# Two of the first four x blocks transposed by DMA instead of the PE, V moved between Q and K of the first quarter, and the range check's matmul moved among the last projections

## The chip, the cores and the metric

The kernel runs on one core of one Trainium2 chip. The metric is the device time of one execution in microseconds (us), as the median of several; lower is better. The executions of one kernel in one set agree within about 0.4%, with a mean granted TensorE clock of 0.997 to 1.000. PE is TensorE, ACT is ScalarE, DVE is VectorE, POOL is GpSimd and SP is SyncE.

## The reference

Two independent problems, A and B, are computed and their results concatenated. Each is sliding-window attention with 2048 tokens, model width 1024, 32 heads of 32, window 256, in bfloat16:

```python
qkv = (x @ wqkv).reshape(B, S, 3, H, Dh).transpose(2, 0, 3, 1, 4)   # S 2048, H 32, Dh 32
scores = einsum("bhqd,bhkd->bhqk", q, k) * Dh ** -0.5
mask = (i - j >= 0) & (i - j < 256)
p = softmax(where(mask, scores, -1e9))
o = einsum("bhqk,bhkd->bhqd", p, v)
return o.transpose(0, 2, 1, 3).reshape(B, S, D) @ wo               # for A and B, then concatenated
```

## The kernel before

The work is a list of 180 *slots*. A slot makes the scores of four (key block, query block) pairs on the PE into one PSUM tile `st` of four banks, and ACT takes the exponential of all of them in one instruction of 1.88 us. The rest of the slot's PE time is filled with P.V products of earlier slots and with *chains*: eight matmuls (or two times eight of half width) of a projection of Q, K, V or of the output. A greedy list in Python decides at build time how much of which chain goes into which slot.

Chains write into two alternating PSUM banks `pp`. When a chain ends, its bank is emptied ("evicted") by ACT or DVE, as a small clock model in the builder chooses:

```python
class _Clock:
    def chain(self):
        self.pe = max(self.pe, self.banks.pop(0))
    def evacuate(self, engines):
        best = min(engines, key=lambda e: max(getattr(self, e), self.pe) + COST[e])
        end = max(getattr(self, best), self.pe + 150.0) + COST[best]
        ...
def evacuate(out, in_, engines=("act", "dve")):          # L188
    if clock.evacuate(engines) == "act":
        nc.scalar.copy(out=out, in_=in_)                 # L190
    else:
        nc.vector.tensor_copy(out=out, in_=in_)
```

Projections need x transposed. The first quarter of x (512 tokens) arrives as rows, in four blocks, and the PE turns each block with eight 128x128 transposes (`flip`); ACT and DVE copy the halves back. Later quarters are transposed by DMA. The start, with filler matmuls (`keep_warm`) while the PE has no data:

```python
for a in range(QB):                                      # QB = 4
    nc.sync.dma_start(out=xrow[a], in_=problems[0][0][a * P:(a + 1) * P, :])
    if a == 1:
        load_wqk(0, 1, nc.sync)
load_wv(0, 0, CT, nc.sync)
new_x(0, 1); load_x(0, 1)                                # next quarter, by DMA transpose
...
keep_warm(6)
flip(0); keep_warm(4); flip(1); keep_warm(3)
first(0, 0)                     # Q of columns 0..255
flip(2); flip(3)
first(1, 0); first(0, 256); first(1, 256)                # K, Q, K
emit(0, chains[0].size)                                  # V of blocks 0, 1
```

A range check guards the softmax without a maximum: bits of all Q and K are or-ed, and at the end one 1x1 matmul sums a flag over the partitions and DVE compares it:

```python
def decide(pool):
    csum = pool.tile([P, 512], F32, name="pp")
    nc.tensor.matmul(csum[0:1, 0:1], lhsT=ones1[:], rhs=okp[:], start=True, stop=True)
    nc.vector.tensor_scalar(out=unsafe_i[:], in0=csum[0:1, 0:1], ...)
```

After the last scores come a few P.V products and some 48 us of output projections alone, each chain of eight taking 1.73 us. I call that the *tail*.

## Time and profile before

| | before |
|---|---|
| median of 3 runs (range) | 609.61 us (609.18 to 610.35) |
| span of the profiled execution | 607.6 us |
| first projection of the second x quarter | 15.92 us |
| start of the last scores | 553.75 us |
| start of the last ACT cast | 602.25 us |

The last three rows cut the span at points that both programs have in common: before the first, all work of quarter 0 and the first scores are done in either program; after the second there remains the tail. So I compare *start* (up to 15.92), *body* (553.75 - 15.92 = 537.83) and *tail* (602.25 - 553.75 = 48.50) one by one.

The busy table, the start's chain of waits, the PE's waits and the check's lines are in the prediction below. Two more views of the kernel before are needed. First, the PE's timeline at the end of the start. The columns are start, length, engine, line, operation, output and inputs, shape, and count; in brackets would stand the idle time before it.

```profile
11.99 1.91 PE L172 MATMUL pp<-wv,xT 128*128 128x256 bf16 x16
13.83 0.40 PE L451 MATMUL st<-qT,kT 32*128 32x384 bf16 x8
14.16 1.92 PE L172 MATMUL pp<-wv,xT 128*128 128x256 bf16 x16
15.92 0.81 PE L172 MATMUL pp<-xT,wqk 128*128 128x512 bf16 x2
```

Nothing stands in brackets: V, the first scores, V again and the second quarter follow one another. The last line is my mark for the end of the start. Secondly, the SP queue's own timeline (the time that the issuing took):

```profile
3.77 8.07 SPq L133 DMA_TRANSPOSE xT<-in_A_x_dram  x1
13.12 6.00 SPq L133 DMA_TRANSPOSE xT<-in_A_x_dram  x1
```

Each of these DMAs transposes 1 MB and held its queue for 6 to 8 us here. The first of them brings the second quarter of x; it landed 10.2 us after its issue, at 14.0, and was wanted at 15.92.

### The profile page before, as it was taken

The page shows a single profiled execution, that of the slowest core. Times are in us where ns is not written, and L with a number is a line of the kernel's source. Part 1 is how long each engine was busy: PE and PEld are TensorE (multiplying, and loading weights), DVE is VectorE, ACT ScalarE, POOL GpSimd, SP SyncE. Part 2 cuts the span into 40 slices and gives each one's busy share as a digit, 9 for nine tenths or more (in the row PEclk, how much of TensorE's full clock was granted, in tenths as well). Part 3 has the DMA queues.
Part 4 walks back from the last instruction along what each step waited for, and adds up shares of the span by engine and source line. Part 5 has one row for each costly group of instructions (what it writes and reads, how often), then busy time and mean ns, then how long its engine had stood idle before and what let it go on. Part 6 is the DMA issues. An engine that isn't in the chain of part 4 may idle for free.

```text
span 607.6 us, 28768 instructions
## 1 busy us (share of the span) xinstructions
PE 593.6 (98%) x12786; PEld 344.3 (57%) x12838; DVE 468.4 (77%) x1199; ACT 441.1 (73%) x376; POOL 326.3 (54%) x630
## 2 busy tenths in 40 slices
PE   8999999999999999999999999999999999999996
PEld 6555466656655756564556756655455665545443
DVE  1677889898898898897888887898888887897200
ACT  3778887788888887877778877777776777785332
POOL 0565666665666666556555565555555655554000
PEclk9999999999999999999999999999999999999999
DMA  9833110111015501442111100112021040113222
GB/s 234 182 92 89 37 38 3 38 38 39 3 38 90 114 14 30 82 101 77 38 37 38 38 4 8 33 37 81 2 68 34 4 106 21 55 58 120 72 79 64
DMA packets 86802, 35.47 MB, mean 58 GB/s; under 512 B 65552, under 2 KB 86160, under 8 KB 86672
## 3 DMA queue, kind: packets, MB, share of 16 engines
q1 hardware_dynamic: 85632, 33.31, 22.2%
q8 instruction: 102, 1.67, 1.2%
q10 hardware_dynamic: 1040, 0.26, 0.2%
q14 instruction: 28, 0.23, 0.1%
HBM read 17.83 MB, written 8.39 MB: 43 GB/s over the span
## 4 chain that ended last, share of the span: by engine, by line
PE 96%; ACT 2%; issue 1%; DMA 1%; ACTq 0%
PE pp L176 44%; PE pp L172 28%; PE acc L513 13%; PE st L451 10%; ACT pt L459 1%; DMA oT<-in_A_x_dram 1%; PE acc L582 0%; PE pp L568 0%; ACT kT L190 0%; ACT vt L190 0%; PE st L582 0%; ACT osb L190 0%; PE pp L805 0%; ACTq L190 0%
## 5 line engine op out<-in xcount | busy, mean ns | idle before, releaser
L459 ACT ACTIVATE pt<-st 128x2048 bf16<-128x2048 f32 x180 | 338.0, 1878 | 91.6 <-PE st L451 73.5
L471 POOL TENSOR_SCALAR_AFFINE_SELECT pt<-pt 128x512 bf16<-128x512 bf16 x224 | 154.5, 690 | 145.7 <-ACT pt L459 143.1
L467 POOL TENSOR_SCALAR_AFFINE_SELECT pt<-pt 128x512 bf16<-128x512 bf16 x256 | 179.2, 701 | 85.8 <-ACT pt L459 85.8
L524 DVE RECIPROCAL rinv<-acc 128x128 f32<-128x128 f32 x128 | 122.0, 953 | 57.0 <-PE acc L513 56.4
L176 PE MATMUL pp<-xT,wqk 128*32 128x512 bf16 x2712 | 163.1, 379 | 0.0
L481 DVE TENSOR_TENSOR both<-pt 128x512 bf16<-128x512 bf16 x224 | 137.1, 651 | 0.0
L176 PEld LDWEIGHTS <-wqk 128*32 128x32 bf16 x2712 | 69.3, 97 | 54.2 <-issue 0.4
L172 PE MATMUL pp<-xT,wqk 128*128 128x512 bf16 (+1 forms) x323 | 76.7, 369 | 4.1 <-issue 2.4
L176 PE MATMUL pp<-wv,xT 128*32 128x256 bf16 x2436 | 75.9, 273 | 0.0
L451 PE MATMUL st<-qT,kT 32*128 32x384 bf16 (+2 forms) x1488 | 71.5, 269 | 0.1
L176 PEld LDWEIGHTS <-xT 128*32 128x32 bf16 x2436 | 63.8, 97 | 6.2
L529 DVE STREAM_SHUFFLE wide<-rinv 128x128 f32<-128x128 f32 x256 | 64.6, 298 | 0.0
L513 PE MATMUL acc<-pt,vt 128*32 128x128 bf16 (+1 forms) x2160 | 63.3, 239 | 0.0
L172 PE MATMUL pp<-wo_sb,oT 128*128 128x512 bf16 (+1 forms) x269 | 59.3, 373 | 1.3 <-issue 0.9
L451 PEld LDWEIGHTS <-kT 32*128 32x128 bf16 x1488 | 22.2, 92 | 64.5 <-issue 63.3
L190 ACT CAST osb<-pp 128x512 bf16<-128x512 f32 (+1 forms) x52 | 30.0, 577 | 39.1 <-PE pp L172 24.4
L531 DVE TENSOR_TENSOR oT<-acc,wide 128x256 bf16<-128x256 f32 x128 | 54.3, 425 | 4.4
L176 PE MATMUL pp<-wo_sb,oT 128*32 128x512 bf16 x952 | 55.6, 379 | 0.0
L172 PEld LDWEIGHTS <-wqk 128*128 128x128 bf16 x362 | 33.4, 98 | 37.0 <-issue 6.8
L172 PE MATMUL pp<-wv,xT 128*128 128x256 bf16 x415 | 50.9, 273 | 1.4 <-ACT kT L190 0.6
L513 PEld LDWEIGHTS <-vt 128*32 128x32 bf16 x2160 | 35.9, 96 | 26.4 <-issue 24.1
L172 PEld LDWEIGHTS <-xT 128*128 128x128 bf16 x415 | 38.9, 98 | 12.0 <-issue 6.1
(46 smaller groups left out, 386.5 us busy)
## 6 DMA issues: line engine op xcount, KB each, us to landing
out_dram<-osb SPq DMA_DIRECT2D x63, 128.0 KB, 1.8
wqk<-in_B_wqkv_dram SPq DMA_DIRECT2D x32, 128.0 KB, 2.5
wqk<-in_A_wqkv_dram SPq DMA_DIRECT2D x24, 128.0 KB, 2.7
wo_sb<-in_A_wo_dram SPq DMA_DIRECT2D x16, 128.0 KB, 2.2
wv<-in_B_wqkv_dram SPq DMA_DIRECT2D x16, 128.0 KB, 2.8
wo_sb<-in_B_wo_dram SPq DMA_DIRECT2D x16, 128.0 KB, 2.4
oT<-in_A_x_dram SPq DMA_DIRECT2D x4, 256.0 KB, 5.4
wv<-in_A_wqkv_dram SPq DMA_DIRECT2D x2, 512.0 KB, 5.9
```

The lines of the kernel that those rows point to most:

```text
L172: nc.tensor.matmul(out[:, lo:hi], lhsT=lhsT, rhs=rhs, start=start, stop=stop, skip_group_check=True)
L176: nc.tensor.matmul(out[c:c + 32, lo:hi], lhsT=lhsT[:, c:c + 32], rhs=rhs, start=start, stop=stop, tile_position=(0, c), skip_group_check=True)
L190: nc.scalar.copy(out=out, in_=in_)
L451: nc.tensor.matmul(st[:, r, a:b, :], lhsT=kT[32 * r:32 * r + 32, j * P:(j + 1) * P], rhs=qT[32 * r:32 * r + 32, q * P:(q + b - a) * P], st ...
L459: nc.scalar.activation(out=pt[:, :, :n, :].rearrange("p r a q -> p r (a q)"), in_=st[:, :, :n, :].rearrange("p r a q -> p r (a q)"), func= ...
L467: nc.gpsimd.affine_select(out=blk, in_=blk, pattern=[[0, 4], [1, P]], compare_op=ALU.is_ge, fill=0.0, base=0, channel_multiplier=-1)
L471: nc.gpsimd.affine_select(out=blk, in_=blk, pattern=[[0, 4], [-1, P]], compare_op=ALU.is_gt, fill=0.0, base=0, channel_multiplier=1)
L481: nc.vector.tensor_tensor(out=both[:, :, h, :], in0=pts[s0][:, :, a0, :], in1=pts[s1][:, :, a1, :], op=ALU.add)
L513: nc.tensor.matmul(acc[32 * r:32 * r + 32, o:o + w_], lhsT=lhsT, rhs=src[:, r, :, :], start=(x == 0), stop=(x == len(moves) - 1), tile_pos ...
L524: nc.vector.reciprocal(out=rinv[:], in_=acc[:, 2 * P:3 * P])
L529: nc.vector.stream_shuffle(out=wide[:, h * P:(h + 1) * P], in_=rinv[:], mask=[16 * h] * 32)
L531: nc.vector.tensor_tensor(out=oTs[(pi, k)][:, t, (p % 2) * 256:(p % 2 + 1) * 256], in0=acc[:, 0:256], in1=wide[:], op=ALU.mult)
```

## The change

The intent is to begin with projections earlier, and to take PE work and evictions out of the start. Blocks 2 and 3 of x come by DMA transpose. Q and K of block 0 follow its flip at once, then those of block 1, then V of blocks 0 and 1, and only then the second halves of Q and K, whose x arrives late. The partial sums of Q and K lie in two banks of one spare `st` tile. The check's matmul goes from the body into the tail.

```diff
-    xrow = [... for a in range(QB)]
+    xrow = [... for a in range(2)]
...
-    for a in range(QB):
+    for a in range(2):
         nc.sync.dma_start(out=xrow[a], in_=problems[0][0][a * P:(a + 1) * P, :])
-        if a == 1:
+        if a == 0:
             load_wqk(0, 1, nc.sync)
     load_wv(0, 0, CT, nc.sync)
+    load_x(0, 0, 2, 2)
...
-    warm = ps_proj.tile([P, 512], F32, name="pp")
+    spare = ps_st.tile([P, 4, SLOTS, P], F32, name="st")[:].rearrange("p r a q -> p r (a q)")
+    warm = spare[:, 1]
...
-    held = [{}, {}]
+    held = [{"pp": spare[:, 2]}, {"pp": spare[:, 3]}]
...
     flip(0)
-    keep_warm(4)
+    keep_warm(3)
+    first(0, P)
     flip(1)
     keep_warm(3)
-    first(0, 0)
-    flip(2)
-    flip(3)
-    first(1, 0)
-    first(0, 256)
-    first(1, 256)
+    first(P, 2 * P)
+    emit(0, chains[0].size)
+    first(2 * P, 4 * P)
+    clock.banks = [clock.pe, clock.pe]
     emit(0, chains[0].size)
...
-        elif now >= sealed + 2 and len(certify) == 1:
-            certify.pop(0)(ps_proj)
-    assert not certify
...
     finish_norm()
+    certify.pop(0)(ps_proj)
     emit(END + 10, float("inf"))
```

In the new version `first(lo, hi)` does Q and then K of those columns.

More of the change, by code (lines that the diff above doesn't have):

```diff
@@ L544, in _fast_path @@
     new_wv(0)
-    xrow = [rows[:, 2 * a:2 * a + 2, :].rearrange("p t n -> p (t n)") for a in range(QB)]
+    xrow = [rows[:, 2 * a:2 * a + 2, :].rearrange("p t n -> p (t n)") for a in range(2)]
     load_wqk(0, 0, nc.scalar)
-    for a in range(QB):
+    for a in range(2):
         nc.sync.dma_start(out=xrow[a], in_=problems[0][0][a * P:(a + 1) * P, :])
-        if a == 1:
+        if a == 0:
             load_wqk(0, 1, nc.sync)
     load_wv(0, 0, CT, nc.sync)
+    load_x(0, 0, 2, 2)
     new_x(0, 1)
@@ L562, in _fast_path @@
             load_wv(1, 0, CT, nc.sync)
-    warm = ps_proj.tile([P, 512], F32, name="pp")
+    spare = ps_st.tile([P, 4, SLOTS, P], F32, name="st")[:].rearrange("p r a q -> p r (a q)")
+    warm = spare[:, 1]
     def keep_warm(n):
         for _ in range(n):
-            nc.tensor.matmul(warm[:], lhsT=blank[:, 0:P], rhs=blank[:, 0:512], start=True, stop=True)
+            nc.tensor.matmul(warm, lhsT=blank[:, 0:P], rhs=blank[:, 0:512], start=True, stop=True)
     keep_warm(6)
-    flips = [ps_acc.tile([P, 512], F32, name="acc") for _ in range(2)]
-    flips = [f[:] for f in flips]
-    flips.append(ps_st.tile([P, 4, SLOTS, P], F32, name="st")[:, 0].rearrange("p a q -> p (a q)"))
-    flips.append(None)
-    held = [{}, {}]
+    flips = [ps_acc.tile([P, 512], F32, name="acc")[:] for _ in range(2)]
+    held = [{"pp": spare[:, 2]}, {"pp": spare[:, 3]}]
     def flip(a):
-        if a == 3:
-            flips[a] = ps_acc.tile([P, 512], F32, name="acc")[:]
         f = flips[a].bitcast(BF16).rearrange("p (ct q) -> p ct q", q=P)
@@ L587, in flip, with first @@
         nc.vector.tensor_copy(out=dst[:, half:, :], in_=f[:, half:, :])
-    def first(which, lo):
-        for _, f in qk_steps(0, which, 0, lo, lo + 256, held[which], last=lo > 0):
-            f()
+    def first(lo, hi):
+        for which in range(2):
+            for _, f in qk_steps(0, which, 0, lo, hi, held[which], last=hi == 512):
+                f()
     flip(0)
-    keep_warm(4)
+    keep_warm(3)
+    first(0, P)
     flip(1)
     keep_warm(3)
-    first(0, 0)
-    flip(2)
-    flip(3)
-    first(1, 0)
-    first(0, 256)
-    first(1, 256)
+    first(P, 2 * P)
+    emit(0, chains[0].size)
+    first(2 * P, 4 * P)
+    clock.banks = [clock.pe, clock.pe]
     emit(0, chains[0].size)
```

## The prediction

> **What bounds the kernel now.** I read, in this order: the busy table and chain of the page; the chain of waits in order of time for the first 30 us; the waits of the PE alone; the timeline where the PE waited; the instructions of the range-check matmul; and the landing times of the DMAs.
>
> ```profile
> PE 593.6 (98%) x12786; PEld 344.3 (57%) x12838; DVE 468.4 (77%) x1199; ACT 441.1 (73%) x376; POOL 326.3 (54%) x630
> ...
> PE 96%; ACT 2%; issue 1%; DMA 1%; ACTq 0%
> ```
> The PE is busy 98% of the span and is 96% of the chain. The PE's work is fixed by the problem, so only three things can move the end: dead PE time at the start, PE waits in the body, and extra PE work. Its idle time is 14.0 us in all (607.6 - 593.6).
>
> ```profile
> 0.80 3.50 DMA oT<-in_A_x_dram
> 4.30 0.04 issue
> 4.34 1.04 PE acc L582 x8
> 5.38 0.90 PE pp L568 x4
> 6.28 0.60 PE acc L582 x8
> 6.89 0.65 PE pp L568 x3
> 7.53 0.03 issue
> 7.56 1.06 PE pp L172 x8
> 8.62 0.45 PE st L582 x8
> 9.06 0.45 PE acc L582 x8
> 9.51 4.39 PE pp L172 x40
> ```
> This is the start (start, length, what): x lands at 4.3 us, L582 turns a block of x (eight 128x128 transposes, 0.45 us when nothing holds them), L568 is filler, L172 is real projection work. Real work starts at 7.56 us, is broken for 0.9 us by blocks 2 and 3, and then never stops.
>
> ```profile
> PE pp L172 <- issue: 3.5, 22, 0.2
> ...
> PE pp L172 <- ACT vt L190: 1.0, 2, 0.5
> PE pp L172 <- ACT kT L190: 0.6, 2, 0.4
> ```
> The PE's own waits (total us, times, longest). The four waits for ACT are real. The 0.16 us "issue" ones I take for missing matmul records: each stands behind a group one matmul shorter than the program has there (9 or 10 for 10 or 11), so nothing is lost in them.
>
> ```profile
> 241.62 0.40 PE L451 MATMUL st<-qT,kT 32*128 32x256 bf16 x8
> ...
> 242.07 1.88 ACT L459 ACTIVATE pt<-st 128x2048 bf16<-128x2048 f32 x1 [0.92 <-PE st L451]
> ...
> 243.84 1.07 ACT L190 CAST vt<-pp 128x512 bf16<-128x512 f32 x2
> ...
> 244.47 0.71 PE L172 MATMUL pp<-wv,xT 128*128 128x256 bf16 x5 [0.49 <-ACT vt L190]
> ```
> One of the four: two projection banks alternate. In a slot that has no P.V work, a chain ends soon after the scores (L451), its eviction stands on ACT behind the 1.88 us exponential, and the next chain but one wants that bank. In all four the PE resumes 2.85 to 2.86 us after the scores started.
>
> **What the Trainium skill says.**
> - "TensorE: Matmul & The Clock Gate", section "Wait — 56ns, not 53.3ns?": warm matmuls start every 55.6 ns at 128 columns and 215.7 ns at 512. The trace agrees: 8 transposes in 0.45 us are 56 ns each, 3 fillers in 0.65 us are 217 ns each.
> - "DMA: Bandwidth & Descriptors", section "Alternative transpose paths": the PE's transpose goes from SBUF to PSUM and needs an identity. So it costs PE time and two evictions, which the DMA's does not. The trace shows both copies: 0.59 us on ACT, then 0.42 us on DVE.
> - The same page, "Issuing engines are not separate DMA queues": all DMAs run on the same 16 engines and interleave. So what counts is bytes in issue order. The trace agrees: from 3 us on the DMA moves 250 to 365 GB/s in every microsecond until 13 us, whoever issued.
>
> **The change, part by part.** All lengths below are from the trace of before; the order is that of the built program.
>
> 1. *Blocks 2 and 3 of x by DMA.* Removed from the PE: 16 transposes at 56 ns = 0.90 us, and one filler of 13 = 0.22 us. In bytes nothing changes (0.5 MB as rows before, 0.5 MB transposed now).
>
> 2. *The new order at the start.* Bytes in issue order: x0, Wq, Wk, x1, Wv, then the half transpose. By the rates of before 1.05 MB have been moved at 6.2 us, 1.57 MB at 7.8, 2.1 MB at 9.6. A landing was about 0.9 us later (Wv, at 2.1 MB, landed 3.29 + 7.1 = 10.4). So I expect Wk at 6.3, x1 at 7.1, Wv at 8.6, the half transpose at 10.4 to 10.6. The PE: flip 0 ends at 5.38 as now; 3 fillers to 6.03; Q of 128 columns waits for ACT's copy (6.01) and DVE's (6.46), ends 6.74; K 8 x 0.056 to 7.19; flip 1 to 7.64; 3 fillers to 8.29; DVE's copy ends 8.72, Q to 9.0, K to 9.45; V of blocks 0 and 1, 16 x 0.108 = 1.73, to 11.2 (Wv is there); Q and K of the other half, 16 x 0.108, to 12.9 (the half transpose is there); V of blocks 2 and 3 to 14.65. Before, the same work was done at 14.16 + 1.73 = 15.89, of which 0.33 was the first scores: 15.56. Gain 0.9 us. All of it is on the path, since the PE runs without a break afterwards. I take -0.95, since the 1.1 us of removed PE work is the ceiling and the two waits for DVE copies give some back.
>
> 3. *The check's matmul among the last projections.* Before:
> ```profile
> 557.06 0.09 PE pp L805
> 557.15 0.60 PE acc L513 x34
> ...
> L806 DVE TENSOR_SCALAR unsafe_i<-pp x1: 145/145/145, 557.2 to 557.2; 1x1 int32<-1x1 f32 x1
> ```
> It cost 0.09 us, because P.V (another bank) followed it. DVE read its bank from 557.2 to 557.35. In the changed program the next instruction is a projection in the *same* bank, waiting for that DVE read: about 0.2 us to DVE's start, 0.145 us there and 0.05 us back = 0.40 us. Net +0.3 us on the path. No wait was removed for it: the PE did not wait at L805 before. The scalar load of the flag on the sync queue (0.52 us) moves too, but stores are not on the path there.
>
> 4. *What the scheduler makes of it.* With V and Q/K reordered and the bank clock reset, the greedy list takes other chains for the first third. Totals of real PE work are equal (same columns of each kind; 55 changes from scores to whole matmuls in both). But I counted the pattern of the four waits: a slot without P.V, an ACT eviction behind the exponential, and its bank wanted in the same slot. The four of before are exactly the four in the trace. In the changed program there are six. Loss of one: resume at 2.86, against 0.33 for scores + 0.216 n, with n the full-width matmuls between; so 2.53 - 0.216 n. Before: n = 10, 8.5, 9, 8.5, so 0.37 + 0.69 + 0.59 + 0.69 = 2.34 us. After: n = 9, 8.5, 10, 9.5, 9, 8.5, so 0.59 + 0.69 + 0.37 + 0.48 + 0.59 + 0.69 = 3.41 us. Net +1.07 us. (The page shows less per wait, since a matmul's modelled end stands some 0.17 us after the next could start.) Slots with P.V have the same shortest gaps in both programs, and the last two thirds are alike.
>
> Sum: 609.61 - 0.95 + 0.3 + 1.05 = 610.0 us.
>
> **The rivals.**
> - *A pure gain at the start.* If the two extra bank waits do not appear (the eviction is ready in time, or the slot runs late anyway), the sum is 609.61 - 0.95 + 0.3 = 609.0. For: most of the change is aimed at the start. Against: the pattern gave a wait four times out of four.
> - *The transfer takes the place of the flips.* The sync engine now issues 1.5 MB of transposes in a row. The first 1 MB took 8.07 us to issue before, the later ones 6.0 and 5.6. If the half transpose lands at 12 instead of 10.5, the PE stands some 0.8 us; if the next x quarter (landed at 3.77 + 10.2 = 14.0, wanted at 15.9 before, now at about 15.0) comes a microsecond late, as much again. Then 610.8 to 611.3. Against: same bytes ahead of it, and the issue was held by the DMA's rate, not by the issuer. I put a fifth on some such wait.
> - *Moving the check frees something.* If the old place of the check disturbed banks or the store queue, it would give up to half a microsecond: 609.5. Against: no PE wait stands near 557 us, and the tail ran at 1.73 us a chain, its full rate, up to 602 us.
>
> **Range and chances.** The start can be off by 0.4, the bank waits by 0.5, a late transfer can add 1, and the median of the kernel before moves by some 0.3 between sets. So 610.0, with 608.9 to 611.0 eight times in ten. 2% is 12 us, as much as nearly all dead PE time of the kernel: neither side is within reach.
>
> **What would show each step right or wrong.** In the timeline: first projection at 6.1 instead of 7.56 us; first scores at 14.6 to 15.1 with all of quarter 0 done, no PE wait for a DMA past 7.2 us. In the PE's waits: six waits for ACT evictions (two more), about 2.3 us shown instead of 1.6. In the tail: one PE gap of about 0.3 us at the check's matmul, ended by DVE. PE busy down by about 1 us. It is wrong if a DMA ends a PE wait at 11 or 15 us, if the six places show no wait, or if the span differs by over 1.5 us either way.

## The result

The changed kernel took 611.86 us (median of 6 runs, 611.55 to 612.43), against 609.76 (6 runs, 609.18 to 610.35) for the kernel before in the same rounds. The ratio is 1.0035, with a 95% interval of 1.0022 to 1.0048. Ratios here are the mean time of one kernel's runs over that of the other's of the same rounds, so they are not quite the ratio of the medians quoted. The kernel is about 2.1 us slower, and the time is above the predicted range.

The page of the changed kernel begins its busy table and its chain as follows:

```profile
PE 599.4 (98%) x12780; PEld 343.5 (56%) x12780; DVE 468.0 (77%) x1196; ACT 440.6 (72%) x375; POOL 324.9 (53%) x630
...
PE 76%; ACT 1%; issue 0%; DVE 0%; ACTq 0%
```

The reader can see little in these two: PE busy rose by 5.8 us where work was taken from it. Part of that is bookkeeping. The many 0.16 us "issue" gaps of before (3.5 us), which I took for missing matmul records, are absent from this trace. So the sum of busy time is no measure of 2 us here, and I went by places.

The PE's own waits, in us total, times, longest:

```profile
PE pp L172 <- ACT vt L190: 1.3, 3, 0.5
PE st L172 <- ACT qT L190: 0.7, 1, 0.7
...
PE pp L172 <- ACT qT L190: 0.4, 1, 0.4
PE pp L172 <- DVE unsafe_i L801: 0.2, 1, 0.2
```

The two lines for `pp` and ACT are four of the six evictions of step 4; the other two, both of K, are a line equal to that of before (0.6 us, two times). The last line is the check in the tail. The second is new and was in no step of the prediction: a projection into `st` that waits for ACT's eviction of Q. Where it stands is shown by the timeline of the start:

```profile
4.51 1.03 PE L579 MATMUL acc<-ident,oT 128*128 128x128 bf16 x8 [0.46 <-DMA oT<-in_A_x_dram]
5.34 1.49 PE L570 MATMUL st<-top 128*128 128x512 bf16 x3
6.62 1.28 PE L172 MATMUL st<-xT,wqk 128*128 128x128 bf16 x16
7.74 0.61 PE L579 MATMUL acc<-ident,oT 128*128 128x128 bf16 x8
...
10.15 1.91 PE L172 MATMUL pp<-wv,xT 128*128 128x256 bf16 x16
11.89 1.04 PE L172 MATMUL st<-xT,wqk 128*128 128x256 bf16 x8
12.97 0.59 ACT L190 CAST qT<-st 128x512 bf16<-128x512 f32 x1 [0.29 <-PE st L172]
13.60 1.03 PE L172 MATMUL st<-xT,wqk 128*128 128x256 bf16 x8 [0.67 <-ACT qT L190]
14.47 1.91 PE L172 MATMUL pp<-wv,xT 128*128 128x256 bf16 x16
16.32 0.40 PE L451 MATMUL st<-qT,kT 32*128 32x384 bf16 x8
```

This view answers to the start of before. Q's second half is issued at 11.89; eight matmuls of 256 columns at 0.108 us fill 0.86 us, so K could start at 12.75. It starts at 13.60, right after ACT's cast of Q (12.97 + 0.59 = 13.56): 0.85 us lost. Q and K lie in different banks, but in one tile, `spare`. In the built program K's matmul waits for the ACT instruction that reads Q's half of that tile.

The tail, in the chain of waits of the changed kernel (start, length, what):

```profile
567.63 3.56 PE pp L172 x16
571.19 0.13 PE pp L800 x2
571.33 0.02 issue
571.35 0.15 DVE unsafe_i L801
571.51 0.04 issue
571.55 0.59 PE pp L172 x2
```

Sixteen matmuls at 0.2157 us end their issue at 567.63 + 3.45 = 571.08, and the next projection starts at 571.55. The check costs 0.47 us there. The SP queue, finally, issues two transposes back to back:

```profile
2.82 10.62 SPq L133 DMA_TRANSPOSE xT<-in_A_x_dram  x2
```

In the DMA views the half transpose landed 8.8 us after its issue, at 11.6, and the second quarter, issued at 8.97, landed 6.6 us later, at 15.6.

By stage:

| | before | changed | difference |
|---|---|---|---|
| start: first projection of quarter 1 | 15.92 | 16.64 | +0.72 |
| body: from there to the last scores | 537.83 | 538.99 | +1.16 |
| tail: to the last ACT cast | 48.50 | 48.99 | +0.49 |

Up to that cast the profiled executions differ by 2.37 us (their spans by 2.6). Below it turns out that the start varies between executions of one order by up to a microsecond, and that before's profiled start was an early one.

### The profile page after: what moved, and what is told of

Read it like the earlier page. It is cut to its first block, busy times and chain, and to the rows that moved or that the text cites. A ratio compares the mean times of both kernels' runs of the same rounds, so it can differ in the third digit from the quotient of the medians.

```text
span 610.2 us, 28698 instructions
## 1 busy us (share of the span) xinstructions
PE 599.4 (98%) x12780; PEld 343.5 (56%) x12780; DVE 468.0 (77%) x1196; ACT 440.6 (72%) x375; POOL 324.9 (53%) x630
## 3 DMA queue, kind: packets, MB, share of 16 engines
q8 instruction: 102, 1.67, 1.2%
## 4 chain that ended last, share of the span: by engine, by line
PE 76%; ACT 1%; issue 0%; DVE 0%; ACTq 0%
PE pp L176 35%; PE pp L172 23%; PE acc L513 11%; PE st L451 7%; ACT pt L459 1%; ACT vt L190 0%; ACT kT L190 0%; ACT osb L190 0%; DVE unsafe_i L801 0%; PE pp L800 0%; ACTq L190 0%
## 5 line engine op out<-in xcount | busy, mean ns | idle before, releaser
L172 PE MATMUL pp<-xT,wqk 128*128 128x512 bf16 x327 | 78.5, 380 | 0.7 <-ACT qT L190 0.4
L176 PE MATMUL pp<-wv,xT 128*32 128x256 bf16 x2348 | 73.5, 273 | 0.1
L176 PEld LDWEIGHTS <-xT 128*32 128x32 bf16 x2348 | 61.4, 97 | 5.8 <-issue 0.3
L172 PE MATMUL pp<-wo_sb,oT 128*128 128x512 bf16 (+1 forms) x282 | 61.4, 373 | 0.2 <-DVE unsafe_i L801 0.2
L172 PE MATMUL pp<-wv,xT 128*128 128x256 bf16 x437 | 53.8, 273 | 1.6 <-ACT vt L190 1.0
L172 PEld LDWEIGHTS <-xT 128*128 128x128 bf16 x437 | 41.3, 98 | 13.1 <-issue 6.1
```

The lines of the kernel that those rows point to most:

```text
L172: nc.tensor.matmul(out[:, lo:hi], lhsT=lhsT, rhs=rhs, start=start, stop=stop, skip_group_check=True)
L176: nc.tensor.matmul(out[c:c + 32, lo:hi], lhsT=lhsT[:, c:c + 32], rhs=rhs, start=start, stop=stop, tile_position=(0, c), skip_group_check=True)
```

## The experiments

Twelve kernels ran in three sets of four, five rounds each (five or six timed runs of each kernel). Each set shares its runs of the kernel before, with medians of 610.12, 609.94 and 609.64 us. All results were correct. The label begins with `a` for a version of the changed kernel and `b` for one of the kernel before.

### Repeating the changed kernel: a_again

No edit.

> The changed kernel once more, unaltered, to have it in the same rounds as the next three. Expected 1.8 to 2.2 us over the kernel before of these rounds. Its profile tells whether the start repeats: K's second half behind the eviction of Q for 0.67 us shown, the half transpose landing at 11.4 to 11.7 us and the next x quarter at 15.3 to 17.0 us (before: 14.0), first scores at 15.9 to 16.4 us.

It took 611.93 us (611.30 to 612.96), ratio 1.0030 (1.0016 to 1.0044). Its start ended at 16.39, its body was 539.15, its tail 48.99. K waits again (0.67 us shown), and so do the six evictions. What was found in one profile holds in a second one; the start is 0.25 us earlier.

### The check alone: a_oldcheck and b_newcheck

```diff
 a_oldcheck, against the changed kernel (b_newcheck is the reverse, on the kernel before)
             certify.pop(0)(top)
+        elif now >= sealed + 2 and len(certify) == 1:
+            certify.pop(0)(ps_proj)
+    assert not certify
...
     finish_norm()
-    certify.pop(0)(ps_proj)
```

> The changed kernel with the check's matmul back at its old place, before a P.V. Theory 1 (the check costs the PE 0.36 us at its new place, 0.09 at its old one): 611.86 - 0.27 = 611.6 us, and no PE wait ended by the flag's read. Rival (the check's place is the main loss, through banks or the store queue): 610.3 us or less. Rival 2 (the wait is absorbed by slack in the tail): 611.86.

> The kernel before with nothing but the check's matmul moved to its new place. Theory 1 (0.36 us there against 0.09): 0.27 us slower than the kernel before of these rounds, one PE wait ended by the flag's read in the tail. Rival (the move costs what the run with the old check place suggested at most, 0.7 us, because the store queue or the banks of the tail are disturbed too): 0.7 us slower.

a_oldcheck: 611.47 us (611.10 to 611.86), ratio 1.0023 (1.0009 to 1.0037); start 16.54, body 539.08, tail 48.50. b_newcheck: 610.31 us (610.23 to 610.89), ratio 1.0006 (0.9994 to 1.0018); start 16.22, body 537.93, tail 48.99. The wait moved with the edit. It is gone from a_oldcheck, and b_newcheck has it:

```profile
PE pp L172 <- DVE unsafe_i L804: 0.2, 1, 0.2
```

The PE's waits show 0.2 us for it, but both tails move by 0.49 us, one down and one up, and both bodies stay as they were. The place of the check is worth 0.49 us in the tails; its old place cost nothing that can be seen in the body. The timed differences, some 0.4 us each way, have the right sign and size but are not clear of noise by themselves.

### K's wait for Q's eviction: a_defer

The evictions of the second halves are issued only when both Q and K are done, so no eviction stands between them.

```diff
-            nc.scalar.copy(out=out, in_=in_)
+            f = lambda: nc.scalar.copy(out=out, in_=in_)
         else:
-            nc.vector.tensor_copy(out=out, in_=in_)
+            f = lambda: nc.vector.tensor_copy(out=out, in_=in_)
+        later.append(f) if later else f()
...
+    later.append(None)
     first(2 * P, 4 * P)
+    later.pop(0)
+    for f in later:
+        f()
+    later.clear()
```

> The changed kernel with the evictions of Q and K of the first quarter both issued after the last K matmul of that quarter, on the same engines; nothing else differs in any engine's order. The wait of K's second half for the eviction of Q (0.67 us shown, 13.60 - 12.75 = 0.85 us of lost PE time) is taken away. Theory 1 (that wait is on the path): 611.86 - 0.85 = 611.0 us, first scores at 15.5 instead of 16.3 us. Rival (the start is lost to the late x block and the slow PE clock, and this wait only moves to the first scores, which need the same evictions): 611.8 us, first scores at 16.2 to 16.4.

612.65 us (611.68 to 612.86), ratio 1.0037 (1.0024 to 1.0051): no gain. Yet the wait is gone. Its timeline:

```profile
11.70 1.91 PE L172 MATMUL st<-xT,wqk 128*128 128x256 bf16 x16
13.44 1.91 PE L172 MATMUL pp<-wv,xT 128*128 128x256 bf16 x16
15.28 0.40 PE L453 MATMUL st<-qT,kT 32*128 32x384 bf16 x8
17.03 0.81 PE L172 MATMUL pp<-xT,wqk 128*128 128x512 bf16 x2 [1.35 <-DMA xT<-in_A_x_dram]
```

Q and K run in one piece, and the first scores start at 15.28 instead of 16.32 (16.16 in a_pick, whose start was as little held up by slow fillers). Then the PE wants the second x quarter at 15.61 and gets it at 17.03: 1.42 us of waiting take the place of 0.85 removed. Neither theory had named this DMA as the one that would show next.

How late it came needs care, because this is one profile, and of the slowest of the five runs. A transfer here marks its landing in 16 parts. Fifteen of them stood by 15.37 us, as early as in the other profiles with a half transpose (15.1 to 15.6 complete), and the sixteenth at 16.99. Only one other profile has such a straggler, a_pe4_defer (fifteen parts by 13.85, the last at 15.45, without any half transpose). Both have this edit; whether the edit causes it, or chance, is not shown. So K's wait is real, and taking it away bought nothing that can be measured; in the profiled run the straggler is what took the gain, and for the four others that is not shown.

### Two blocks by DMA, without the new order: b_dma2

```diff
-    xrow = [... for a in range(QB)]
+    xrow = [... for a in range(2)]
-    for a in range(QB):
+    for a in range(2):
         nc.sync.dma_start(out=xrow[a], ...)
...
     load_wv(0, 0, CT, nc.sync)
+    load_x(0, 0, 2, 2)
...
-    flip(2)
-    flip(3)
```

> The kernel before with nothing but blocks 2 and 3 of x turned by the transposing DMA, the order of its projections kept (no V between). Theory 1 (the half transpose lands at 11.4 to 11.7 us, so the second half of Q, due at 9.3 us, waits 2.2 us; 0.9 us of flips are saved): 1.2 to 1.6 us slower than the kernel before, one PE wait of about 2 us ended by the x transpose, the same four waits for ACT evictions. Rival (the transposed half comes with the bytes, at 9.6 to 10.4 us, as predicted): same as before to 0.3 us faster.

611.05 us (610.90 to 611.65), ratio 1.0018 (1.0006 to 1.0030). The wait is on the line where block 2 is first used:

```profile
11.71 1.91 PE L172 MATMUL pp<-xT,wqk 128*128 128x256 bf16 x16 [2.20 <-DMA xT<-in_A_x_dram]
```

The PE stood 2.20 us until the half transpose landed (11.6); the start ended at 17.38. Body (537.86) and tail (48.50) are those of before. So here the transfer cost more than the flips that it replaces. The change's new order puts other work ahead of it.

### The new order, without the DMA: a_pe4_defer

The changed order with a_defer's edit, and with all four blocks turned on the PE.

```diff
 a_defer, and
-    for a in range(2):
+    for a in range(QB):
         nc.sync.dma_start(out=xrow[a], ...)
...
-    load_x(0, 0, 2, 2)
...
     first(P, 2 * P)
+    flip(2)
+    flip(3)
     emit(0, chains[0].size)
```

> The changed kernel with all four x blocks turned on the PE, in the new order (V between), and with the evictions of Q and K both after the last K matmul. It has the order of the changed kernel without its two start waits: no wait of K for Q's eviction, and the next x quarter lands at 14.0 us again. Theory 1 (the order itself gains nothing, the gain was to be the 0.9 us of flips): first scores at 16.2 to 16.6 us, first work on the next quarter at 16.6 to 16.9 without a wait for a DMA, so 612.0 to 612.4 us where the kernel before has 609.9. Rival (the order is good and the DMA turn spoils it): first work on the next quarter before 16.0 us and 611.4 us or less.

611.41 us (610.98 to 611.70), ratio 1.0030 (1.0016 to 1.0044). The first scores start at 15.88, and the second quarter follows at once:

```profile
15.88 0.40 PE L453 MATMUL st<-qT,kT 32*128 32x384 bf16 x8
16.21 1.47 PE L172 MATMUL pp<-xT,wqk 128*128 128x512 bf16 x5
```

The second quarter landed at 15.5 here, without a half transpose ahead of it (the straggler told of above), and no DMA wait stands there. But the start ends at 16.21, no earlier than an average start of before (16.13, see below); the body took 538.72, the tail 48.99. Neither text has it quite; this lies between them. In this profile the order, freed of its two waits, gains nothing.

### The fillers after the first flip: a_nofill

```diff
     flip(0)
-    keep_warm(3)
     first(0, P)
```

> The changed kernel without the three filler matmuls after the first flip. In five of six profiles of the changed kernel and its variants these ran at half pace (0.43 us each instead of 0.216) and held the first Q matmul to 6.3 to 6.6 us although x was there at 6.0 to 6.2. Theory 1 (the fillers are lost PE time when the clock is late): 0.3 to 0.4 us faster than the changed kernel, 611.5 us where the kernel before has 609.9. Rival (without them the PE stays at half pace for longer, and Q and K at 128 columns take the loss): 611.9 or more, with the first 16 matmuls of Q and K taking over 1.4 us.

612.49 us (612.05 to 612.97), ratio 1.0049 (1.0035 to 1.0063), beside 1.0030 to 1.0035 of the changed kernel. It is slower by some 0.9 us, but the intervals overlap, so that the fillers earn their place is likely and not shown. Nor is it settled why: its one profile caught an execution in which the matmuls reached full pace early, with a start of 16.43, a body of 538.96 and a tail of 48.99, none of them longer than in a_again. A clock that stays low longer in the other executions would fit, but no trace shows it.

### The bank waits given to DVE: b_dve4 and a_dve6

The evictions that the PE waited for are moved to DVE by their number.

```diff
-        if clock.evacuate(engines) == "act":
+        best = clock.evacuate(engines)
+        turn[0] += 1
+        if best == "act" and turn[0] - 1 not in (24, 31, 37, 52, 89, 96):   # b_dve4: (27, 55, 89, 96)
             nc.scalar.copy(out=out, in_=in_)
```

> The kernel before, with the four evictions that its PE waited for on DVE instead of ACT, PE order the same. Theory 1: 609.76 - (0.37 + 0.69 + 0.59 + 0.69 = 2.34) = 607.4 us, up to 608.0 if DVE is late for some. Then the two extra waits of the changed kernel account for 1.07 us of its loss. Rival (such a wait is no loss): 609.8.

> The changed kernel with six projection evictions, those that the PE waited for behind an exponential, issued on DVE instead of ACT; the scheduler's own clock still books them on ACT, so the PE order is the same. Theory 1 (each of the six is PE time lost, 2.53 us - 0.216 n, 3.4 us in all): 611.86 - 3.4 = 608.5 us if DVE is in time for all, up to 609.3 if its queue makes some late; PE waits for ACT evictions gone from the body. Rival (what the PE loses there it gains later, because later waits shrink, or the evictions on DVE hold up P.V instead): 611.3 to 611.9.

b_dve4: 609.15 us (608.84 to 609.85), ratio 0.9984 (0.9970 to 0.9997); body 537.32, so 0.55 us less than the mean of the unaltered bodies of before (537.87, from before, b_newcheck and b_dma2). a_dve6: 610.60 us (610.30 to 610.96), ratio 1.0010 (0.9996 to 1.0023); body 537.61, 1.46 us less than the mean of the unaltered changed bodies (539.07, from the changed kernel, a_again and a_oldcheck). Less than half of what I expected, and the PE's waits of a_dve6 tell why:

```profile
PE pp L172 <- DVE vt L195: 1.1, 2, 0.7
```

The ACT waits are gone, but DVE was itself busy and came late. As a test it shows that the waits cost time, not how much. It does bear on the *difference* between the two kernels: the bodies lie 1.20 us apart unaltered, and 0.29 apart with these evictions on DVE.

### The bank waits avoided by order: b_finish, b_pick and a_pick

Finishing the running chain *before* the scores lets its eviction reach ACT ahead of the exponential. b_finish does so by rule, the other two only in chosen slots, three and five of them; what follows such a slot is scheduled anew, and in the built programs the pattern of the waits is gone.

```diff
         whole[0] = not (due and due[0][0] <= now)
+        # b_finish
+        left = sum(ns for ns, _ in current)
+        if whole[0] and 0 < left <= 3 * NS_MM:
+            emit(now, left)
+        # a_pick; b_pick has (20, 73, 79, -1)
+        if now in (17, 23, 41, 73, 79, -1):
+            emit(now, sum(ns for ns, _ in current))
         session(now)
```

> The kernel before with one rule added to its scheduler: in a slot without P.V, a projection chain with at most three full-width matmuls left is finished before the scores, so its eviction stands ahead of the exponential on ACT. In the built program the pattern of the four waits (bank wanted in the slot in which an ACT eviction stands behind the exponential, no P.V) is gone: none left. Theory 1: 609.76 - 2.34 on the first chip, so 2.3 us faster than the kernel before of these rounds, 1.5 if the later exponentials cost something. Rival (the exponential, now 0.6 us later in those slots, holds up the next scores instead): same time as before.

> The kernel before with its scheduler told the same in three slots (20, 73, 79); the pattern is gone from the built program. Theory 1: 2.34 us faster than the kernel before of these rounds, so 607.6 us where that has 609.9. Rival: 0.8 us faster, as with the general rule. With theory 1 right in both runs, the difference of the two is what the start and the check make: 608.5 - 607.6 = 0.9 us (check 0.5, start 0.2 to 0.4).

> The changed kernel with its scheduler told to finish the current projection chain before the scores in five of the 180 slots (17, 23, 41, 73, 79), those where the six PE waits for ACT evictions stood; all other slots keep their rule. In the built program the pattern is gone. Theory 1 (the six waits cost 3.4 us, and are only there because a chain ends just after the scores): 611.9 - 3.4 = 608.5 us on rounds where the kernel before has 609.9; no PE wait for an ACT eviction in the body. Rival (as with the general rule: half of it comes back as later exponentials): 610.2.

| | median (range) | ratio (95%) | body | against the unaltered body |
|---|---|---|---|---|
| b_finish | 609.14 (608.46 to 610.96) | 0.9990 (0.9974 to 1.0007) | 537.04 | -0.83 |
| b_pick | 607.63 (607.38 to 608.37) | 0.9971 (0.9958 to 0.9985) | 536.02 | -1.85 |
| a_pick | 609.62 (609.31 to 610.10) | 1.0000 (0.9986 to 1.0014) | 537.18 | -1.89 |

In none of the three does the PE wait in the body for an ACT eviction of its `pp` bank. In b_finish one moved to the scores:

```profile
PE st L451 <- ACT vt L190: 0.3, 1, 0.3
```

b_pick recovers 1.85 of the 2.34 us that the prediction put on the four waits. By the medians it is 2.0 us faster than the kernel before (1.8 by the ratio), and 4.2 us below the changed kernel's 611.86 of other rounds, so it beats both. a_pick recovers 1.89 of 3.41. New waits stand in its timeline:

```profile
65.23 0.40 PE L451 MATMUL st<-qT,kT 32*128 32x128 bf16 x8 [0.26 <-issue]
65.98 0.58 ACT L190 CAST qT<-pp 128x512 bf16<-128x512 f32 x1 [1.22 <-DVE top L184]
66.46 1.88 ACT L459 ACTIVATE pt<-st 128x2048 bf16<-128x2048 f32 x1
68.40 0.40 PE L451 MATMUL st<-qT,kT 32*128 32x384 bf16 x8 [0.29 <-ACT pt L459]
```

Slot 17's scores are done at 65.6, but the exponential starts only at 66.46: the eviction that was put ahead of it stands first on ACT, and itself waited until 65.98, with DVE's or of the range check named as what released it. There is one `st` tile, so the next slot's scores wait for that exponential, 0.29 us. Another loss in a_pick is a pause inside a P.V group near 268.8 us, for which the trace names no releaser ("issue").

Brackets understate a loss, because a matmul's modelled end stands after the next one could start. Counted instead from the starts of the matmuls (the gap between two, less the usual gap between two of their kinds), a_pick lost 0.32 us before slot 17's scores, 0.36 behind that exponential and 0.50 in the pause. That is 1.18 us, and its body stays 1.16 us above b_pick's. b_pick has one new gap, 0.32 us before the scores at 222.9 (a_pick has the same one). The four waits that it lost count 2.22 us in this way, so 1.90 should be left, and 1.85 was measured.

## Why the prediction was wrong

The verdict at 2% and the bound (the PE, with nothing else near it) were right. The time was 1.9 us above the prediction and 0.9 above the range. Step by step:

**Step 1, the flips taken away:** the removal itself is right, and worth nothing alone. In b_dma2 the same removal brought a 2.20 us wait.

**Step 2, the order of the start, is the step that failed:** "first scores at 14.6 to 15.1", gain 0.95. They started at 16.32 in the profiled run. For the whole start I compare means of profiles with an unaltered start: before 15.92, 16.69, 16.22, 16.11, 15.71, mean 16.13 (before, b_dve4, b_newcheck, b_finish, b_pick); changed 16.64, 16.39, 16.54, 16.25, 16.49, mean 16.46 (the changed kernel, a_again, a_oldcheck, a_dve6, a_pick). So the start became 0.33 us *longer* instead of 0.95 shorter: 1.28 us of error. With five profiles each and this spread the 0.33 itself is not sure; that the 0.95 is missing is.

The spread goes with the PE's pace. Each kept trace has a record of full granted clock, which begins between 4.0 and 7.1 us (the view by stretches shows 1.00 throughout and doesn't tell this). The starts of before follow it: 15.71 with the record from 4.5 us, 15.92 from 5.3, 16.69 from 7.1. With a late record the two orders are alike (16.69 in b_dve4, 16.64 in the changed kernel, 16.54 in a_oldcheck, all from 7.1). With an early one the changed order does not follow: 16.25 in a_dve6 (from 5.4), 16.49 in a_pick (from 4.0). So on these ten profiles the new order loses where the PE is at full pace early.

Against the predicted instants, three things went wrong:

- *An overlooked wait.* I let K follow Q at once at 256 columns each, "16 x 0.108, to 12.9". K waited for Q's eviction, 0.85 us. This is shown by the timeline, by its repetition, and by a_defer, where it vanished.
- *Late data behind it.* "The next x quarter (landed at 14.0 ...)" was kept at its old place, and the half transpose at "10.4 to 10.6". They landed at 11.6 and 15.6, and in the other profiles of the changed start at 11.3 to 11.7 and at 15.1 to 15.4, in a_defer at 17.0. Even without K's wait the start could not end before the second quarter is there, 0.1 to 0.6 us later than the 15.0 predicted. The rule "bytes in issue order" failed: from 3 to 10 us the DMA moved 1.88 MB, and 1.89 in b_dma2, which has the half transpose too, against 2.10 before and 2.12 in a_pe4_defer, which have it not. Between 10 and 12 us it moved 166 and 187 GB/s, where it had moved 249 and 290 before, with one transpose ending and the next beginning.
- *The first flip to the second.* I had flip 1 at 7.19; it came at 7.74. In the profiled run the three fillers took 6.62 - 5.34 = 1.28 us, 0.43 each instead of 0.216, and the record of full clock begins only at 7.07. Where it began earlier, x1 set the limit, which I had at 7.1: in a_pick x1 landed at 7.45 and flip 1 came at 7.49, in a_dve6 at 7.29 and 7.33, in a_pe4_defer at 7.19 and 7.23. So 0.04 to 0.55 us are gone here, by execution.

Of the 1.67 us between the predicted 14.65 and the measured 16.32, then, 0.55 lie before flip 1, 0.85 in K's wait, and the rest in small gaps.

**Step 3, the check:** the mechanism is right (the wait for DVE's read, one gap in the tail), and its size too small: predicted +0.3, measured +0.49 by the tails of a_oldcheck and b_newcheck. The PE loses 0.47 us at the new place, where I had 0.40, and the old place gave back nothing visible of its 0.09.

**Step 4, the bank waits:** right in mechanism and size. Six waits were predicted and six appeared, 2.28 us shown in the timeline against the predicted 2.3. One of them, with no P.V in its slot as predicted:

```profile
85.59 0.71 PE L172 MATMUL pp<-wv,xT 128*128 128x256 bf16 x5 [0.52 <-ACT vt L190]
```

A least-squares fit of slot lengths to the matmul columns of each kind leaves the slots in question over by 0.38, 0.69, 0.62 and 0.65 before (sum 2.34, predicted 2.34), and by 0.63, 0.71, 0.42, 0.50, 0.64 and 0.66 after (sum 3.56, predicted 3.41). The fit's working is not shown here; counted straight from the starts of the matmuls, as for a_pick above, the four and the six come to 2.22 and 3.25 us. The bodies differ by 539.07 - 537.87 = 1.20 us, predicted 1.07. That such waits cost this time is borne out by b_pick, which removes them and gains 2.0 us, and that the two extra ones make the difference, by the pair on DVE, which leaves 0.29 of the 1.20. a_pick and b_pick do not show the latter: each came down by the same 1.9, since a_pick met new losses. No experiment got all of the 2.34 or 3.41 us back.

The sum of what was measured is 0.33 + 1.20 + 0.49 = 2.0 us, and the timed differences are 2.1 (first measurement) and 2.0 (a_again; 1.8 by its ratio).

**The rivals:** the second one, a transfer that takes the place of the flips, was nearest. It said that the half transpose might land at 12 and the next quarter a microsecond late; they landed at 11.6 and 1.6 us late. I gave it a fifth. In the changed kernel as it stands, though, no PE wait for a DMA is shown there: K's wait comes first, and the PE asks for the second quarter only at 16.64. The pure gain, and the gain from moving the check, did not appear.

**What stays open:** whether and why a_nofill is 0.9 us slower; what held the last sixteenth of the second quarter in a_defer and a_pe4_defer; why the DMA is slower with the half transpose; and the pause of 0.50 us in a_pick.

## What to carry to other kernels

When a start is reordered, list every wait of the built program for the moved instructions, evictions of other banks of the same tile included, and carry forward the landing time of *every* later transfer on that queue, not only of the one that was added. Removing a wait pays only as far as the next data are there; ask what each engine will stand on next, as on the second x quarter in a_defer. In a kernel whose PE is 98% busy, a few waits of 0.5 us behind another engine's long instruction were worth more than the reordering of the start: pulling the chain's end ahead of the scores in three slots brought 2.0 us, more than the change was meant to.

## What the Trainium skill lacked or had wrong

- "DMA: Bandwidth & Descriptors", section "Issuing engines are not separate DMA queues": I took from it that bytes in issue order are enough to place a landing. That is my step, not the page's, and it misled: with the same bytes ahead of it, the second quarter landed at 15.6 instead of 14.0, and the rate fell to 166 and 187 GB/s between the two transposes, from 249 and 290. I found no page that says what a second transposing DMA costs behind the first on one queue; the runs do not tell what causes the dip.
- The same page, section "Alternative transpose paths": it says what each path needs, but not when a transpose by DMA lands. Rates for a transposing DMA by itself stand in other places of the skill; a landing time with other loads ahead was not found. Here 0.5 MB landed 8.8 us after its issue, and the PE's flip of a quarter of a megabyte took 0.45 us of PE time once the rows were there.
- "TensorE: Matmul & The Clock Gate", section "What's actually happening": it says that the number of slow matmuls at the start varies from run to run, as the window is free-running. The runs agree: fillers took 0.43 us each in some profiles where others had 0.216, and the record of full clock begins anywhere from 4.0 to 7.1 us, and starts of one unaltered order ended between 15.71 and 16.69. The section gives the ramp as under 1% of a typical kernel span and advises against fitting to a count; for a change worth 0.2% that spread is as large as the effect, and one profile of each kernel does not decide.
- No page was found that warns of a wait between two banks of one PSUM tile. It lies in the built program: Q and K shared one tile and K waited, 0.85 us; in the kernel before they had a tile each, and no such wait stands there. That the wait is kept by tile is read from these two programs only.
